# Batch 0's first-stage results: moved inside SBUF instead of through memory, and x laid out in two runs

## The chip, the cores and the metric

The kernel runs on one core of a Trainium2 chip (trn2). The metric is the device time of one execution in microseconds (us); lower is better. The kernel before takes 2643.61 us, the median of three runs from 2640.65 to 2645.09. The core has a matrix engine (PE, with PEld for its weight loads), three elementwise engines (DVE, ACT, POOL) and SP, which only issues DMA transfers; ACT can issue them too.

## The reference

The input x is 8 batches of 3008 rows of 256 numbers. Cut to what matters, the reference computes:

```python
X = np.fft.rfft(x, axis=1)
Yr = Xr @ w_r - Xi @ w_i + b_r
Yi = Xr @ w_i + Xi @ w_r + b_i
Y = sign(Y) * max(|Y| - 0.01, 0)          # on Yr and Yi apart
y = np.fft.irfft(Y, n=3008, axis=1)       # 24064 rows of 256
h = y @ moe_w_in                          # 256 to 2048
out = (h * clip(h + 3, 0, 6) / 6) @ moe_w_out   # 2048 to 256
```

So every batch passes a transform along its rows, a complex 256x256 product with a threshold, the transform back, and all rows then pass a two-layer network whose weights come as 64-bit floats.

## The kernel before, in words

**The transform** is split as 3008 = 64 x 47. `stage1(b)` does the 47-point part on TensorE. Its tiles hold 120 partitions: five of the 64 indices n1 by 24 values of k (`J` = 5, `NK` = 24, `R47` = 120). The 64 indices come in seven sets (`SEGS`): six of ten (two groups of five side by side, 512 columns) and one of four (96 partitions, 256 columns), which goes first. For each set `load` fetches the rows of x and their mirrored rows into `xin`, one vector operation forms the sum `e`, one the difference, and one matmul each (c = 0 and c = 1) gives a result that ACT copies into the tile `a` (line 303). Line 305 writes `a` to `scr1`, a buffer in memory whose axes are (c, n1), k and the 256 columns.

`middle(b)` takes the same data the other way round: for each pair g of two k values (12 pairs) `load` reads `bt`, 128 partitions (c, n1) by 2 x 256, back out of `scr1` (line 367), and a piece `f` of the 64-point transform (line 368). `s2` multiplies (line 376) and splits the result into `X` (line 131 in `split`, ACT the high part, DVE the low), `s3` does the complex product with bias and threshold, four small transfers `zt` swap halves (line 439), `s5` transforms back, and `scr2` takes the result (line 456). `segment` does the 47-point part back, `prepare` makes the operands `yb` of the network.

**The network** is done in chunks of 512 rows and eight bands of 256 hidden columns (`nf` = 8), in the main loop at the end: `phase_a` to `phase_d` (seven products per block, line 137), `gate`, and `down` (line 631). From the second batch on, `stage1` and `middle` run in small steps between these blocks. Batch 0 has nothing to hide behind: its `stage1` and `middle` stand ahead of the main loop.

**The weights** of a band are decoded on the chip from 64-bit words: `in_band(f)` and `out_band(f)` load `st` (line 178) and work on DVE, ACT and POOL (lines 190 to 222). `in_band(f)` writes its seven 128x128 blocks, as a high and a low part, into entry f of the two tiles `w_in_hi` and `w_in_lo` (`win_s`). Five bands are asked for beside `middle(0)` (`EARLY`), the others behind it with working space borrowed from tiles of `middle` (`LATE`; `bt` is one).

**What sets the order.** The program's order gives each engine's instructions a priority, and a scheduler then places them by times of its own, so the rows of an engine do not stand as the functions are written. Each engine works its row strictly in turn. Transfers issued by SP and by ACT share eight semaphores: an issue waits until the transfer eight places before it has landed. A tile with one buffer (`a` in batch 0 has seven under different names) is written again only when its last reader is done.

Of the kernel before, what the change touches and what calls it, by code (L numbers as in the profile page):

```python
# [9 lines left out]
F32 = mybir.dt.float32  # L10
F32R = mybir.dt.float32r
# [10 lines left out]
B, S, D, FF = 8, 3008, 256, 2048  # L22
N1, N2 = 64, 47
NK = N2 // 2 + 1
LAM = 0.01
P = 128

J = 5
SEGS = tuple((n1, min(2 * J, N1 - n1)) for n1 in range(0, N1, 2 * J))
R47 = J * NK  # L30
# [70 lines left out]
def spectral_ffn(ctx: ExitStack, tc: tile.TileContext, x, w_r, w_i, bias, w_in, w_out, f47, f64, g64, sgn, out):  # L101
    nc = tc.nc
    const = ctx.enter_context(tc.tile_pool(name="const", bufs=1))
    sb = ctx.enter_context(tc.tile_pool(name="sb", bufs=1))
    dram = ctx.enter_context(tc.tile_pool(name="dram", bufs=2, space=DRAM))
# [8 lines left out]
    def space(shape, dt, name, tag=None):  # L114
        tag = tag or name
        return sb.tile(shape, dt, name=name, tag=tag, bufs=depth.get(tag, 1))

    def twin(shape, dt, name, tag=None):

        t = space([P, 2, *shape[1:]], dt, name, tag)  # L120
        return t[:, 0], t[:, 1]
# [6 lines left out]
    def split(hi, lo, src, on=None):  # L128

        nc.scalar.copy(out=hi, in_=src)  # L130
        (on or nc.vector).tensor_tensor(out=lo, in0=src, in1=hi.bitcast(F32), op=ALU.subtract)  # L131

    def product(ps, terms, start=True, stop=True, more=False):

        todo = [p for (ah, al), (bh, bl) in terms for p in ((al, bh), (ah, bl), (ah, bh))]
        for n, (a, b) in enumerate(todo):
            nc.tensor.matmul(  # L137
                out=ps,
                lhsT=a,
                rhs=b,  # L140
                start=start and n == 0,
                stop=stop and n == len(todo) - 1,
                skip_group_check=more,
            )
# [13 lines left out]
    nf = NFT // 2  # L158
# [5 lines left out]

    win_s = [const.tile([P, nf, 7, P], F32R, name="w_in_" + t) for t in ("hi", "lo")]
    wout_s = [const.tile([P, NFT * D], F32R, name="w_out_" + t) for t in ("hi", "lo")]

    top = const.tile([P, 2], F32, name="top")  # L170
# [3 lines left out]
    def decode(src, cut, tags):  # L174


        st = space([P, 2, 256, 2], I32, "st", tags[0])
        nc.sync.dma_start(out=st.rearrange("p a c w -> p a (c w)"), in_=cut(src, 2))
        yield
        high = st[:, :, :, 1]  # L180
        e = space([P, 2, 256], I32, "e", tags[1])
        m, r = (
            twin([P, 2, 256], I32, "m", tags[2])
            if len(tags) == 3
            else [space([P, 2, 256], I32, n, t) for n, t in zip("mr", tags[2:])]
        )
        mf, rf = m.bitcast(F32), r.bitcast(F32)
        v, s = nc.vector, nc.scalar

        v.tensor_scalar(out=e, in0=high, scalar1=20, scalar2=0x7FF, op0=ALU.arith_shift_right, op1=ALU.bitwise_and)  # L190
        v.tensor_scalar(out=m, in0=high, scalar1=0xFFFFF, scalar2=0xFFFFF, op0=ALU.bitwise_and, op1=ALU.bitwise_and)
        yield
        s.activation(out=rf, in_=e, func=AF.Relu, bias=top[:, :1], scale=-1.0)
        s.activation(out=e, in_=rf, func=AF.Relu, bias=top[:, 1:], scale=-(2.0**23))
        v.scalar_tensor_tensor(out=e, in0=high, scalar=-(1 << 31), in1=e, op0=ALU.bitwise_and, op1=ALU.bitwise_or)
        halves = st.rearrange("p a c w -> p (a c w)").bitcast(U16).rearrange("p (a c w) -> p a c w", a=2, w=4)
        s.activation(out=rf, in_=halves[:, :, :, 1], func=AF.Copy, bias=1.0, scale=2.0**-36)
        yield
        v.scalar_tensor_tensor(out=mf, in0=m, scalar=2.0**-20, in1=rf, op0=ALU.mult, op1=ALU.add)
        nc.gpsimd.tensor_tensor(out=mf, in0=mf, in1=e.bitcast(F32), op=ALU.mult)  # L200
        return mf, e.bitcast(F32)

    def in_band(f, tags):
        def cut(t, words):
            v = t.rearrange("p (h c) -> p h c", h=2)
            return v[:, :, f * 256 * words : (f + 1) * 256 * words]

        w, s = yield from decode(w_in, cut, tags)
        s = s.rearrange("p a (b c) -> p (a b) c", b=2)
        a11, a12, a21, a22 = w[:, 0, :P], w[:, 1, :P], w[:, 0, P:], w[:, 1, P:]  # L210
        for to, a, b, op in (
            (0, a21, a22, ALU.add),
            (1, s[:, 0], a11, ALU.subtract),
            (2, a11, a21, ALU.subtract),
            (3, a12, s[:, 1], ALU.subtract),
        ):
            nc.gpsimd.tensor_tensor(out=s[:, to], in0=a, in1=b, op=op)
        yield
        hi, lo = (t[:, f] for t in win_s)
        split(hi[:, :2], lo[:, :2], w[:, :, :P])  # L220
        split(hi[:, 2], lo[:, 2], a22)
        split(hi[:, 3:], lo[:, 3:], s)
# [39 lines left out]
    scr1, scr2 = {}, {}  # L262

    def stage1(b):
        scr1[b] = dram.tile([2, N1, NK, D], F32, name="scr1")
        sets = SEGS[-1:] + SEGS[:-1]
        xins = {}

        def load(i):
            n1, n = sets[i]  # L270
            rows, w = (R47, 2 * D) if n == 2 * J else (n * NK, D)
            tag = ("xin", "gs", None, "gs", None, "raw", "raw")[i] if b == 0 else "xin"
            if tag == "gs":
                xins[i], xins[i + 1] = twin([P, 2, 2 * D], F32, "xin", tag)
            elif tag:
                xins[i] = space([P, 2, 2 * D], F32, "xin", tag)
            at = n1 // J * 2 * D
            src = x[b, :rows, at : at + 2 * w].rearrange("p (s c) -> p s c", s=2)
            nc.sync.dma_start(out=xins[i][:rows, :, :w], in_=src)
            return rows, w  # L280

        shapes = [load(i) for i in range(len(sets))] if b == 0 else [load(0)]
        for i, (n1, n) in enumerate(sets):
            rows, w = shapes[i]
            xin = xins.pop(i)
            plus, minus = xin[:rows, 0, :w], xin[:rows, 1, :w]
            e = space([P, 2 * D], F32, "e", "r" if b == 0 else "e")[:rows, :w]
            (nc.vector if b == 0 else nc.gpsimd).tensor_tensor(out=e, in0=plus, in1=minus, op=ALU.add)  # L288
            (nc.vector if b == 0 else nc.gpsimd).tensor_tensor(out=plus, in0=plus, in1=minus, op=ALU.subtract)
            for c, src in enumerate((e, plus)):  # L290
                q = 2 * i + c
                if b == 0:
                    ps = room(c == 1)
                    turns = f47_s[2][:rows, c * R47 : c * R47 + rows]
                    nc.tensor.matmul(out=ps[:rows, :w], lhsT=turns, rhs=src, start=True, stop=True)
                else:
                    xs = [t[:rows, :w] for t in twin([P, 2 * D], F32R, "xs")]
                    split(*xs, src, nc.vector if b == 1 else nc.gpsimd)
                    yield
                    ps = room()  # L300
                    product(ps[:rows, :w], [([t[:rows, c * R47 : c * R47 + rows] for t in f47_s[:2]], xs)])
                a = space([P, 2 * D], F32, "a", ("a", "h", "z", "h", "xs", "h", "X")[q % 7] if b == 0 else "a")[:rows, :w]
                nc.scalar.copy(out=a, in_=ps[:rows, :w])
                dst = scr1[b][c, n1 : n1 + n].rearrange("(g j) k d -> (j k) g d", g=w // D)
                (nc.sync if b else nc.scalar).dma_start(out=dst, in_=a.rearrange("p (g d) -> p g d", d=D))
                if c and b and i + 1 < len(sets):
                    shapes.append(load(i + 1))
                yield
# [26 lines left out]
    for i, _ in enumerate(stage1(0)):  # L335
        if i == 7:
            r, k = [loaded(w, P, 2 * D, n, "yb") for w, n in ((w_r, "w_r"), (w_i, "w_i"))]
# [14 lines left out]

    def middle(b):
        scr2[b] = dram.tile([2, N1, NK, D], F32, name="scr2")
        src = scr1[b].rearrange("c n k d -> (c n) k d")
        dst = scr2[b].rearrange("c n k d -> (c n) k d")
        NG = NK // 2
        LAG = (1, 2, 3) if b else (2, 5, 5)
        bt, xs, zs = {}, {}, {}
# [3 lines left out]
            return tags[0 if b else g % 3]  # L363

        def load(g):
            bt[g] = space([P, 2, D], F32, "bt"), space([P, 2, P], F32, "f64")
            nc.sync.dma_start(out=bt[g][0], in_=src[:, 2 * g : 2 * g + 2, :])
            nc.sync.dma_start(out=bt[g][1], in_=f64.rearrange("p (k c) -> p k c", c=P)[:, 2 * g : 2 * g + 2])

        def s2(g):  # L370
# [170 lines left out]
    WEIGHT = {1: 0, 2: 1, 3: 6, 4: 2, 5: 3, 6: 4, 7: 5}  # L541
    yb = {}
# [16 lines left out]

    def block(i, n, ps, start):  # L560
        c, f = units[i]
        product(ps, [(tuple(t[:, f, WEIGHT[n]] for t in win_s), yb[c, n])], start=start, more=True)

    def kept(i, n, ps):
        t = keep[i, n] = space([P, H], F32, n)
# [122 lines left out]
    for c in range(1, NC):  # L688
        g = prepare(c)
# [23 lines left out]
    n = len(units)  # L713
# [75 lines left out]
```

## Time and profile before

| | |
|---|---|
| median of three runs | 2643.61 us |
| the profiled execution: its own time, its span | 2643.59 us, 2641.8 us |
| PE busy, mean granted TensorE clock | 2562.4 us (97%), 0.988 |
| busy time of DVE, ACT, POOL | 1975.7, 1820.1, 796.0 us |
| last result of batch 0's stage 1 leaves ACT | 31.66 us |
| first matmul of `middle(0)` | 41.45 us |
| first `X` product of `middle(0)` | 49.98 us |
| end of its last `X` product | 107.1 us |

Times in the trace count from the start of the span. In a row of the timeline the first number is the start, the second the duration, and a square bracket tells how long the engine sat idle before and what ended that; `SPq` and `ACTq` are transfers being issued. A window row gives each engine's busy time in a stretch, then the granted clock, the busy share of the 16 DMA engines, and GB/s.

### The profile page before, as it was taken

To read this page: it belongs to the slowest core of one execution; us is meant where nothing else is said; L and a number is where in the kernel's file an instruction comes from. 1 tells how busy PE (TensorE), PEld (TensorE's weight loads), DVE (VectorE), ACT (ScalarE), POOL (GpSimd) and SP (SyncE) were. 2 spreads that over 40 slices of the span, in tenths; PEclk is the share of its full clock that TensorE was granted. 3 is DMA by queue.
4 is the path that set the end of the run, shared out by engine and by line. 5 is a ranking of instruction groups with operands and counts; after the bars stand their busy time and mean duration, and the time that the engine had idled before them with its cause. 6 is when DMAs were issued, how large, how long until landed. Compare 5 with 4: busy or idle time off the path is not lost.

```text
span 2641.8 us, 44527 instructions
## 1 busy us (share of the span) xinstructions
PE 2562.4 (97%) x16406; PEld 2291.9 (87%) x16406; DVE 1975.7 (75%) x3186; ACT 1820.1 (69%) x3592; POOL 796.0 (30%) x749
## 2 busy tenths in 40 slices
PE   5789999999999999999999999999999999999999
PEld 3577998988898998988898998999889889898887
DVE  7786886877677777777777777777777777666766
ACT  5476677767667777766776777677777666676766
POOL 2263334443233332233323333233321121121210
PEclk8889999999999999999999999999999999999999
DMA  7623333332223321323213322233221111100000
GB/s 216 191 79 93 103 104 94 113 107 75 59 60 96 88 69 48 85 78 90 73 49 86 88 76 63 76 84 84 63 79 58 50 53 53 43 26 30 12 17 17
DMA packets 150178, 199.98 MB, mean 76 GB/s; under 512 B 16847, under 2 KB 104135, under 8 KB 149959
## 3 DMA queue, kind: packets, MB, share of 16 engines
q1 hardware_dynamic: 146675, 193.98, 25.4%
q10 hardware_dynamic: 3284, 3.15, 0.4%
q8 instruction: 129, 2.11, 0.3%
q14 instruction: 90, 0.74, 0.1%
HBM read 97.45 MB, written 74.97 MB: 65 GB/s over the span
## 4 chain that ended last, share of the span: by engine, by line
PE 84%; DVE 4%; ACT 4%; DMA 2%; POOL 2%; issue 2%; SPq 0%; ACTq 0%; POOLq 0%; DVEq 0%
PE po L631 36%; PE pb L137 17%; PE ps_a L137 11%; PE pc L137 9%; PE pd L137 4%; PE ps_a L505 3%; PE ps_a L376 3%; ACT gs L130 1%; DMA xin<-in_x 1%; DVE r L610 1%; ACT r L608 1%; DVE gs L131 1%; POOL e L288 1%; DVE h L572 1%; POOL yb L131 0%
## 5 line engine op out<-in xcount | busy, mean ns | idle before, releaser
L631 PE MATMUL po<-gs,w_out_hi 128*128 128x512 f32 x3008 | 1006.5, 396 | 0.0
L610 DVE SCALAR_TENSOR_TENSOR r<-r,h 128x1024 f32<-128x1024 f32 x376 | 486.9, 1295 | 267.7 <-ACT r L608 265.9
L631 PEld LDWEIGHTS po<-gs,w_out_hi 128*128 128x128 f32 x3008 | 541.3, 188 | 85.5
L631 PE MATMUL po<-gs,w_out_lo 128*128 128x512 f32 x1504 | 601.9, 400 | 5.9 <-ACT gs L130 3.3
L608 ACT ACTIVATE r<-h,three 128x1024 f32<-128x1024 f32 x376 | 434.3, 1155 | 214.6 <-DVE h L572 211.6
L137 PE MATMUL pb<-yb,w_in_hi 128*128 128x256 f32 x3008 | 571.6, 279 | 2.5 <-POOL yb L131 2.5
L131 DVE TENSOR_TENSOR gs<-r,gs 128x1024 fp32r<-128x1024 f32 x376 | 484.4, 1288 | 80.7 <-ACT gs L130 78.8
L137 PEld LDWEIGHTS pb<-yb,w_in_hi 128*128 128x128 f32 x3008 | 461.0, 189 | 22.5 <-POOL yb L131 2.7
L130 ACT CAST gs<-r 128x1024 fp32r<-128x1024 f32 x376 | 395.8, 1053 | 92.5 <-DVE r L610 89.5
L572 DVE TENSOR_TENSOR h<-pc,u 128x256 f32<-128x256 f32 x752 | 315.1, 419 | 175.3 <-PE pc L137 160.1
L131 POOL TENSOR_TENSOR yb<-T,yb 128x256 fp32r<-128x256 f32 x188 | 181.0, 969 | 859.4 <-ACT yb L130 841.6
L137 PE MATMUL pb<-yb,w_in_lo 128*128 128x256 f32 x1504 | 431.3, 288 | 4.6 <-ACT p L567 1.6
L567 ACT COPY u<-pb 128x256 f32<-128x256 f32 x752 | 277.8, 373 | 121.5 <-PE pb L137 103.8
L631 PEld LDWEIGHTS po<-gs,w_out_lo 128*128 128x128 f32 x1504 | 284.0, 189 | 63.3 <-ACT gs L130 14.5
L137 PEld LDWEIGHTS pb<-yb,w_in_lo 128*128 128x128 f32 x1504 | 284.3, 189 | 29.7 <-ACT h L601 4.1
L137 PE MATMUL pc<-yb,w_in_hi 128*128 128x256 f32 x1504 | 297.6, 279 | 0.8 <-POOL yb L131 0.8
L137 PEld LDWEIGHTS pc<-yb,w_in_hi 128*128 128x128 f32 x1504 | 230.7, 189 | 13.3 <-POOL yb L131 1.1
L137 PE MATMUL pc<-yb,w_in_lo 128*128 128x256 f32 x752 | 219.0, 291 | 5.5 <-DVE h L572 4.9
L567 ACT COPY p<-pb 128x256 f32<-128x256 f32 x376 | 139.9, 372 | 80.9 <-PE pb L137 78.6
L601 ACT COPY h<-pb 128x256 f32<-128x256 f32 x376 | 140.5, 374 | 57.4 <-PE pb L137 55.4
L572 DVE TENSOR_TENSOR h<-pd,p 128x256 f32<-128x256 f32 x376 | 156.7, 417 | 14.9 <-ACT p L567 10.2
L137 PEld LDWEIGHTS pc<-yb,w_in_lo 128*128 128x128 f32 x752 | 142.1, 189 | 21.7 <-DVE h L572 7.9
(125 smaller groups left out, 3928.9 us busy)
## 6 DMA issues: line engine op xcount, KB each, us to landing
bt<-scr SPq DMA_DIRECT2D x96, 256.0 KB, 2.9
scr<-pt SPq DMA_DIRECT2D x96, 256.0 KB, 2.4
zt<-tc SPq DMA_DIRECT2D x376, 64.0 KB, 2.0
out<-ot SPq DMA_DIRECT2D x94, 256.0 KB, 2.3
xin<-in_x SPq DMA_DIRECT2D x48, 480.0 KB, 4.8
qt<-scr SPq DMA_DIRECT2D x96, 240.0 KB, 3.5
scr<-a SPq DMA_DIRECT2D x84, 240.0 KB, 2.5
f<-in_f SPq DMA_DIRECT2D x96, 128.0 KB, 2.8
```

The costliest lines, as they stand in the source:

```text
L130: nc.scalar.copy(out=hi, in_=src)
L131: (on or nc.vector).tensor_tensor(out=lo, in0=src, in1=hi.bitcast(F32), op=ALU.subtract)
L137: nc.tensor.matmul(out=ps, lhsT=a, rhs=b, start=start and n == 0, stop=stop and n == len(todo) - 1, skip_group_check=more,)
L288: (nc.vector if b == 0 else nc.gpsimd).tensor_tensor(out=e, in0=plus, in1=minus, op=ALU.add)
L376: nc.tensor.matmul(out=psv[:, dh, :, u, :], lhsT=data[:, u, dh * P : (dh + 1) * P], rhs=f[:, u, :], start=True, stop=True,)
L505: nc.tensor.matmul(out=ps[:, cs * w + g * rows : cs * w + (g + 1) * rows], lhsT=qt[:rows, cs, g, dh * P : (dh + 1) * P], rhs=f47_s[2][:row ...
L567: nc.scalar.copy(out=t, in_=ps)
L572: nc.vector.tensor_tensor(out=to, in0=ps, in1=keep.pop((i, n)), op=ALU.add)
L601: nc.scalar.copy(out=hs[i][:, 1, :H], in_=pb)
L608: nc.scalar.activation(out=r, in_=h, func=AF.Relu, bias=three, scale=1.0)
L610: nc.vector.scalar_tensor_tensor(out=r, in0=r, scalar=6.0, in1=h, op0=ALU.min, op1=ALU.mult)
L631: nc.tensor.matmul(out=pos[dh], lhsT=w[:, ft * D + dh * P : ft * D + (dh + 1) * P], rhs=g[:, low, u], start=f == 0 and u == 0 and which == ...
```

## The change

For batch 0 there is no `scr1` any more. `win_s` becomes one tile of 16 entries, `w_in`: the high part of band f is entry f, its low part entry 15 - f. Entries 4 to 10 (high parts of bands 4 to 7, low parts of 7, 6 and 5) are viewed as `spread`, 128 partitions by 24 by 256, in the layout that `bt` had. Each result `a` of `stage1(0)` is sent there within SBUF: one transfer for each group of five n1, its source 120 partitions of 1 KB, its destination 5 partitions of 24 KB. The first group goes out on ACT's queue, the second on SP's. `s2` of batch 0 multiplies straight from `spread`; the twelve loads `bt` of batch 0 go. The other batches keep `scr1` and `bt`.

Apart from that, x lies in memory as two runs (rows, mirrored rows) of 16 x 256 for each of the 120 rows, so that a load of 120 x 1024 takes two pieces of 2 KB from each row, where it took one of 4 KB. This holds for all batches.

```diff
-    win_s = [const.tile([P, nf, 7, P], F32R, name="w_in_" + t) for t in ("hi", "lo")]
+    win_t = const.tile([P, 2 * nf, 7, P], F32R, name="w_in")
+    win_s = [[win_t[:, f] for f in range(nf)], [win_t[:, 2 * nf - 1 - f] for f in range(nf)]]
+    spread = win_t[:, nf // 2 : nf // 2 + 7].rearrange("p f s c -> p (f s c)").bitcast(F32)
+    spread = spread[:, : NK * D].rearrange("p (k d) -> p k d", d=D)
...
-            at = n1 // J * 2 * D
-            src = x[b, :rows, at : at + 2 * w].rearrange("p (s c) -> p s c", s=2)
+            at = n1 // J * D
+            src = x[b, :rows].rearrange("p (s c) -> p s c", s=2)[:, :, at : at + w]
...
-                (nc.sync if b else nc.scalar).dma_start(out=dst, in_=a.rearrange("p (g d) -> p g d", d=D))
+                if b:
...
+                else:
+                    for g in range(w // D):
+                        at = c * N1 + n1 + g * J
+                        queue = nc.sync if g else nc.scalar
+                        queue.dma_start(out=spread[at : at + rows // NK], in_=a[:, g * D : (g + 1) * D])
...
-            bt[g] = space([P, 2, D], F32, "bt"), space([P, 2, P], F32, "f64")
-            nc.sync.dma_start(out=bt[g][0], in_=src[:, 2 * g : 2 * g + 2, :])
+            bt[g] = space([P, 2, D], F32, "bt") if b else spread[:, 2 * g : 2 * g + 2], space([P, 2, P], F32, "f64")
+            if b:
+                nc.sync.dma_start(out=bt[g][0], in_=src[:, 2 * g : 2 * g + 2, :])
```

The instructions move with it. SP's row from the load of `bias` to the first `bt` loads stands like this before; `f` are pieces of the 64-point transform, `st` the 64-bit weights:

```order
L338 DMA bias<-in_bias 128x512
L339 DMA sgn<-in_sgn 128x24
L151 DMA g_all<-in_g 128x128
L368 DMA f_232<-in_f 128x256
L368 DMA f_236<-in_f 128x256
L178 DMA st<-in_w_in 128x2x512 x4
L178 DMA st<-in_w_out 128x1024
L367 DMA bt<-scr_95 128x512 x2
```

And in the changed kernel, over the same stretch (lines are 3 to 11 higher there):

```order
L348 DMA bias<-in_bias 128x512
L315 DMA w_in<-a 5x24x256
L349 DMA sgn<-in_sgn 128x24
L315 DMA w_in<-a 5x24x256 x2
L151 DMA g_all<-in_g 128x128
L315 DMA w_in<-a 5x24x256 x3
L379 DMA f_241<-in_f 128x256
L315 DMA w_in<-a 5x24x256 x4
L379 DMA f_243<-in_f 128x256
L181 DMA st<-in_w_in 128x2x512
L315 DMA w_in<-a 5x24x256 x2
L181 DMA st<-in_w_in 128x2x512 x3
```

The two `bt` loads are gone, and twelve moves into `spread` have come in, ten of them ahead of the first load of weights and all twelve ahead of the second.

DVE's row up to the first `X` of `middle(0)`, the last rows before it, in the kernel before (`e`, `m`, `w_in` are steps of the decoding):

```order
L190 TENSOR_SCALAR e<-st 128x512
L191 TENSOR_SCALAR m<-st 128x512
L199 SCALAR_TENSOR_TENSOR m<-m 128x512
L131 TENSOR_TENSOR w_in_lo<-m,w_in_hi 128x256
L131 TENSOR_TENSOR w_in_lo<-m,w_in_hi 128x128
L195 SCALAR_TENSOR_TENSOR e<-st,e 128x512
L190 TENSOR_SCALAR e<-st 128x512
L191 TENSOR_SCALAR m<-st 128x512
L199 SCALAR_TENSOR_TENSOR m<-m,r 128x512
L131 TENSOR_TENSOR X<-pb,X 128x2x256
```

In the changed kernel the rows from the last weight split of stage 1 (`w_i_lo`) to the first `X` are these:

```order
L131 TENSOR_TENSOR w_i_lo<-cst,w_i_hi 128x512
L193 TENSOR_SCALAR e<-st 128x512
L194 TENSOR_SCALAR m<-st 128x512
L198 SCALAR_TENSOR_TENSOR e<-st,e 128x512
L202 SCALAR_TENSOR_TENSOR m<-m,r 128x512
L193 TENSOR_SCALAR e<-st 128x512
L194 TENSOR_SCALAR m<-st 128x512
L131 TENSOR_TENSOR X<-pb,X 128x2x256
```

Before, 22 decoding instructions stand between `w_i_lo` and the first `X` (and one ahead of `w_i_lo`); now six do, so that the first `X` is the 33rd instruction of DVE's row where it was the 50th, and the twelfth and last `X` of `middle(0)` is the 121st where it was the 111th. Of the decoding, ten instructions fewer are left behind that last `X`.

More of the change, by code (lines that the diff above doesn't have):

```diff
@@ L218, in in_band @@
         yield
-        hi, lo = (t[:, f] for t in win_s)
+        hi, lo = (t[f] for t in win_s)
         split(hi[:, :2], lo[:, :2], w[:, :, :P])
@@ L264, in stage1 @@
     def stage1(b):
-        scr1[b] = dram.tile([2, N1, NK, D], F32, name="scr1")
+        if b:
+            scr1[b] = dram.tile([2, N1, NK, D], F32, name="scr1")
         sets = SEGS[-1:] + SEGS[:-1]
@@ L303, in stage1 @@
                 nc.scalar.copy(out=a, in_=ps[:rows, :w])
-                dst = scr1[b][c, n1 : n1 + n].rearrange("(g j) k d -> (j k) g d", g=w // D)
-                (nc.sync if b else nc.scalar).dma_start(out=dst, in_=a.rearrange("p (g d) -> p g d", d=D))
+                if b:
+                    dst = scr1[b][c, n1 : n1 + n].rearrange("(g j) k d -> (j k) g d", g=w // D)
+                    nc.sync.dma_start(out=dst, in_=a.rearrange("p (g d) -> p g d", d=D))
+                else:
[3 more added lines that the diff above has]
+                        queue.dma_start(out=spread[at : at + rows // NK], in_=a[:, g * D : (g + 1) * D])
                 if c and b and i + 1 < len(sets):
@@ L354, in middle @@
         scr2[b] = dram.tile([2, N1, NK, D], F32, name="scr2")
-        src = scr1[b].rearrange("c n k d -> (c n) k d")
+        src = scr1[b].rearrange("c n k d -> (c n) k d") if b else None
         dst = scr2[b].rearrange("c n k d -> (c n) k d")
@@ L365, in load @@
         def load(g):
-            bt[g] = space([P, 2, D], F32, "bt"), space([P, 2, P], F32, "f64")
-            nc.sync.dma_start(out=bt[g][0], in_=src[:, 2 * g : 2 * g + 2, :])
+            bt[g] = space([P, 2, D], F32, "bt") if b else spread[:, 2 * g : 2 * g + 2], space([P, 2, P], F32, "f64")
+            if b:
+                nc.sync.dma_start(out=bt[g][0], in_=src[:, 2 * g : 2 * g + 2, :])
             nc.sync.dma_start(out=bt[g][1], in_=f64.rearrange("p (k c) -> p k c", c=P)[:, 2 * g : 2 * g + 2])
@@ L561, in block @@
         c, f = units[i]
-        product(ps, [(tuple(t[:, f, WEIGHT[n]] for t in win_s), yb[c, n])], start=start, more=True)
+        product(ps, [(tuple(t[f][:, WEIGHT[n]] for t in win_s), yb[c, n])], start=start, more=True)
     def kept(i, n, ps):
@@ L759 @@
     half = half.reshape(B, 2, 13, R47, D).transpose(0, 3, 2, 1, 4)
-    pairs = half[:, :, :12].reshape(B, R47, 6, 2, 2, D).transpose(0, 1, 2, 4, 3, 5)
-    xp = np.zeros((B, R47, 32 * D), np.float32)
-    xp[:, :, : 24 * D] = pairs.reshape(B, R47, 24 * D)
-    xp[:, :, 24 * D : 26 * D] = half[:, :, 12].reshape(B, R47, 2 * D)
+    xp = np.zeros((B, R47, 2, 16, D), np.float32)
+    xp[:, :, :, :13] = half.transpose(0, 1, 3, 2, 4)
+    xp = xp.reshape(B, R47, 32 * D)
     pos = positions()
```

## The prediction

> **What bounds the kernel now.** I read the page first, for where PE is not busy.
>
> ```profile
> span 2641.8 us, 44527 instructions
> PE 2562.4 (97%) x16406; PEld 2291.9 (87%) x16406; DVE 1975.7 (75%) x3186; ACT 1820.1 (69%) x3592; POOL 796.0 (30%) x749
> PE   5789999999999999999999999999999999999999
> DMA  7623333332223321323213322233221111100000
> PE 84%; DVE 4%; ACT 4%; DMA 2%; POOL 2%; issue 2%; SPq 0%; ACTq 0%; POOLq 0%; DVEq 0%
> ```
>
> PE carries the chain, and its gaps stand in the first three of 40 slices, where the DMA engines are busiest too. The windows give the stages; the columns are length, busy time of PE, PEld, DVE, ACT and POOL with counts, granted clock, DMA share and GB/s.
>
> ```profile
> 4.00:16.00 12.00, 9.45 (x14) 3.74 (x14) 6.50 (x11) 1.32 (x3) 0.00 (x0) 1.00 0.99 243
> 34.00:38.00 4.00, 0.00 (x0) 0.00 (x0) 3.78 (x6) 2.87 (x6) 2.24 (x3) 0.50 1.06 382
> 49.00:102.00 53.00, 48.81 (x350) 44.44 (x351) 38.04 (x63) 24.58 (x46) 8.83 (x9) 0.95 0.54 161
> 102.00:165.00 63.00, 38.83 (x186) 31.31 (x184) 57.38 (x97) 41.68 (x87) 42.94 (x44) 0.73 0.47 137
> 300.00:2600.00 2300.00, 2288.73 (x14836) 2062.31 (x14835) 1726.97 (x2797) 1616.20 (x3197) 690.64 (x640) 1.00 0.24 69
> ```
>
> From 300 us on PE is busy for 2288.73 of 2300 us. Nothing that the change does to other engines there can gain more than that rest of 0.5%, and a delay ahead of it reaches the end in full. Before 38 us the transfers are full (share 0.99 and 1.06). From 49 to 102 us `middle(0)` runs, PE-bound with 48.81 of 53; from 102 to 165 us DVE bounds with 57.38 of 63.
>
> The start's chain is read from the timeline, in rows of ACT, SP, PE and DVE:
>
> ```profile
> 11.53 0.59 ACT L303 COPY a<-ps_a 120x512 f32<-120x512 f32 x1 [3.98 <-PE pb L295]
> 18.38 0.57 ACTq L305 DMA_DIRECT2D scr<-a  x1
> 19.00 0.58 ACT L303 COPY a<-pb 120x512 f32<-120x512 f32 x1 [6.88 <-DMA cst<-in_w_r]
> 19.43 13.75 SPq L178 DMA_DIRECT2D st<-in_w_in  x4
> 31.07 0.59 ACT L303 COPY a<-pb 120x512 f32<-120x512 f32 x1
> 37.23 0.81 SPq L367 DMA_DIRECT2D bt<-scr  x2
> 41.45 3.75 PE L376 MATMUL pb<-f,bt 128*128 128x128 f32 x16 [12.30 <-ACT m L197]
> 45.55 0.57 ACT L130 CAST X<-pb 128x512 fp32r<-128x512 f32 x1
> 49.25 0.68 DVE L131 TENSOR_TENSOR X<-pb,X 128x512 fp32r<-128x512 f32 x1
> 49.98 0.58 PE L137 MATMUL ps_a<-w_r_hi,X 128*128 128x256 f32 x1 [4.78 <-DVE X L131]
> ```
>
> The last result leaves ACT at 31.66; its write to memory lands where `bt` may be issued, 37.23; the first `bt` lands, and `s2` starts at 41.45. The releaser in its bracket is ACT's, but ACT was done with that by 40.93, so it was `bt`. So memory costs 41.45 - 31.66 = 9.8 us on this path, which the change attacks. Then PE waits 4.78 us until DVE, busy decoding, comes to the first `X` at 49.25.
>
> **The change part by part.** *The moves themselves.* These rows give the transfers' sizes and times, first the totals of ACT's queue (packets, MB), then KB of one and median us to landing:
>
> ```profile
> q10 hardware_dynamic: 3284, 3.15, 0.4%
> zt<-tc SPq DMA_DIRECT2D x376, 64.0 KB, 2.0
> st<-in_w_in SPq DMA_DIRECT2D x8, 512.0 KB, 5.3
> st<-in_w_out SPq DMA_DIRECT2D x8, 512.0 KB, 4.1
> scr<-a ACTq DMA_DIRECT2D x12, 240.0 KB, 5.0
> scr<-a ACTq DMA_DIRECT2D x2, 96.0 KB, 7.7
> ```
>
> ```profile
> bt<-scr SPq DMA_DIRECT2D x2, 256.0 KB, 4.3
> ```
>
> The 14 writes on ACT's queue are 12 of 240 KB and 2 of 96 KB in pieces of 1 KB, 12 x 240 + 2 x 96 = 3072 packets. The row has 3284; the 212 left are 12 x 15 + 2 x 16. So I read that a transfer closes with one packet for each engine that it uses, and that one of 120 rows uses 15 engines and one of 96 uses 16, equal shares of whole rows. A move into `spread` has a destination of only 5 rows, so that equal shares of whole rows leave it 5 engines of 16. The Trainium skill says the same in "DMA: Bandwidth & Descriptors", section "Why a DMA increments its semaphore by 16 and not by 1": the number of engines is the largest up to 16 that divides both sides' slowest dimension. By that rule, 5 and 120 give 5; the 15 and 16 above agree with it, and no transfer with so short a side is in this trace.
>
> The moves carry the same 3.15 MB (24 of 120 KB, 2 of 96 KB). On 5 engines that is 0.63 MB each. The rate of one engine is bounded by two windows: 382 GB/s / 16 = 23.9 GB/s at 34 to 38 us, when writes of `a` and loads of weights run, and 243 / 16 = 15.2 GB/s at 4 to 16 us, when x is loaded into 120 rows. So the moves take between 0.63 / 23.9, 26 us, and 0.63 / 15.2, 41 us. I take 41: the moves, like the loads of x, write into SBUF with engines that sit close together, and `a` went into memory. They start near 14.5: the first result of full size is ready at 12.1, and the same engines are loading x until about 17. With zt's 2.0 us for the last landing, `s2` starts at 14.5 + 41.4 + 2 = 58 instead of 41.45: +16.5, between +1.5 (at 23.9) and more than 27 (a rival, below). The 9.8 us that went through memory are gone in this, and what is late next is the moves themselves.
>
> *SP's and ACT's rows.* Twelve moves stand on SP's row, all ahead of the second load of weights, and each waits for ACT's copy and for one of the eight transfers in flight. So the weights, loaded from 19.43 on before, come after 45 us or so. Who waits is DVE with the decoding; that is priced in the next step. The moves ask for no more issues than the `bt` and line-305 transfers that go (26 for 14 + 12); an issue in this form costs more, as the weights show:
>
> ```profile
> L178 SPq DMA_DIRECT2D st<-in_w_in x8: 540/578/672, 19.4 to 136.6; - x8
> L178 SPq DMA_DIRECT2D st<-in_w_out x8: 328/338/393, 34.9 to 139.6; - x8
> ```
>
> 26 x 0.24 us is 6 us over two queues, which lies under 41 us of transfer: nothing, unless the moves are quick.
>
> *DVE's row.* The first `X` is now the 33rd instruction instead of the 50th. So the 4.78 us that PE waited fall to a cast and a split, 0.57 + 0.68 and a little for the hand-over, 1.5: -3.3. The decoding that stood before it moves behind it: between the first and the last `X` stand 47 decoding instructions instead of 20. At 38.04 / 63 = 0.60 us the 27 more are 16 us, DVE 54 us in a stretch in which PE has 49. The row is no longer covered by PE: between +1 (54 for 53) and +16 (none of it covered); I take +4, as the 15 us that DVE idled there hold nearly all of it.
>
> *The tail.* From 102 to 165 us DVE bounds, and ten decoding instructions fewer are left there (43 for 53): 10 x 57.38 / 97 = 5.9 us at most, 0 at least; I take -4.
>
> *x in 2 KB pieces.* The weights again: 512 KB in 2 KB pieces land in 5.3 us, in 4 KB pieces in 4.1. A load of x, 480 KB, would be up to 1.1 us later. At the start x is limited by rate (seven loads, 3.0 MB, at 243 GB/s), and later POOL, with 690.64 busy of 2300 us, waits for it. The bounds are +9 (eight waits for x on the chain, 1.1 each) and -2 (should short pieces go faster at the start); I take 0.
>
> The sum, against the profiled execution's own 2643.59 us (its span of 2641.8 and 1.8 around it; the median of the runs is 2643.61): +16.5 - 3.3 + 4 - 4 = +13.2, **2656.8 us**.
>
> **The rivals.** *A, the moves are hidden and the kernel is faster.* If short destinations don't confine a move, it lands like `zt` in about 2 us and the chain is the copies': 31.66 + 0.6 for an issue + 2.0, `s2` at 34.3. That is -7.1, and with -3.3 for the first `X` -10.4, 2633.2 us (the +4 and -4 cancel here too). For it: `zt` moves within SBUF in 2.0 us. Against: `zt` has 64 rows on both sides, and the count of closing packets ties engines to rows. It decides if the last move lands before about 38 us.
>
> *B, five engines at full rate.* The moves take 26 us, `s2` starts at 43: +1.5 - 3.3 = -1.8, 2641.8 us, no change that counts. For it: `a` was read at that rate at 34 to 38 us. Against: there the writes went to memory.
>
> *C, the five rows crowd each other.* The five rows of a move are neighbours. If a pair of moves (ACT's and SP's) goes one after the other, each pair in 4.3 us like `bt` in the busy start, 12 x 4.3 = 52 us, `s2` starts at 68: +27 - 3.3 = +23.7, 2667.3 us. For it: loads into 120 rows reached 243 GB/s with the engines at 0.99, when 382 was to be had elsewhere, so the place of the writing matters. Against: the two moves of a pair go to different rows. The Trainium skill bears on this in "SBUF — State Buffer", section "Door 1: The DMA port swizzle (why `[64,N]` ≈ `[32,N]`)": bandwidth depends on how many of 16 ports the partitions reach, and four neighbouring partitions share a port. By its 436 GB/s over 16 ports, four rows of 24 KB take 3.6 us, and 12 pairs 43 us, an estimate that lies between my forecast and C; the 243 against 382 agrees with it, but no row shows four writers in one place.
>
> **How the numbers follow.** The forecast (moves at x's rate, end between 2650 and 2662) has 0.43, C 0.20, B 0.17, A 0.20. About 0.2% (5.3 us) is what a measurement of this kernel can tell from no change. Slower by more than that are the forecast and C, 0.63; within it B, 0.17; faster A, 0.20. The range leaves out most of A and C's upper end: 2638 to 2672 us. As cases of both signs count, the forecast's own range is 2650 to 2662.
>
> **What would show it.** In the changed kernel's profile: the moves `w_in<-a` with a landing well above 5 us, a DMA share below 0.9 between 20 and 50 us (few engines at work), closing packets of 5 a move; the first matmul of line 387 near 58 us; DVE idle before the first `X`, then busy nearly throughout until the last; PE's gain or loss all ahead of 170 us, and 300 us to the end as long as before. Wrong would be the forecast if the moves land in 2 to 3 us and line 387 starts before 40, or if the loop behind 300 us changes its length.

## The result, and the profile after

The changed kernel takes 2670.97 us, the median of runs from 2668.46 to 2673.80; the kernel before, beside it, 2644.35 (2640.65 to 2645.44). The ratio is 1.0103, with a 95% interval of 1.0086 to 1.0121: 26.6 us slower, where 13.2 were forecast. That is outside the forecast's own range of 2650 to 2662 us, and nearer to rival C's 2667.3 than to the forecast's 2656.8. The profiled execution took 2668.46 us.

From the page: its span, busy times, the slices of PE and of the DMA engines, and ACT's queue.

```profile
span 2666.6 us, 44529 instructions
PE 2566.7 (96%) x16406; PEld 2292.8 (86%) x16406; DVE 1972.5 (74%) x3186; ACT 1819.5 (68%) x3592; POOL 783.5 (29%) x749
PE   3779999999999999999999999999999999999999
DMA  5533333333222322223213322133212111101000
q10 hardware_dynamic: 1700, 1.67, 0.2%
```

The span is 24.8 us longer. ACT's queue carries 12 moves of 120 packets and 2 of 96, 1632; the 68 that are left are 12 x 5 + 2 x 4. So a move into five rows uses five engines. The windows show them at work and the stages behind:

```profile
20.00:50.00 30.00, 9.24 (x10) 2.88 (x10) 5.63 (x9) 8.09 (x16) 0.00 (x0) 0.50 0.40 117
34.00:38.00 4.00, 0.98 (x2) 0.00 (x0) 0.57 (x1) 0.00 (x0) 0.00 (x0) 0.50 0.33 97
52.00:56.00 4.00, 0.00 (x0) 0.00 (x0) 0.76 (x2) 0.50 (x1) 0.00 (x0) 0.50 1.04 255
62.80:122.60 59.80, 49.90 (x359) 45.46 (x359) 50.93 (x90) 37.57 (x72) 23.42 (x23) 0.93 0.48 141
122.60:150.10 27.50, 9.73 (x40) 5.27 (x39) 21.00 (x41) 12.90 (x26) 10.97 (x14) 0.68 0.53 164
300.00:2600.00 2300.00, 2287.32 (x14822) 2059.95 (x14821) 1728.47 (x2800) 1611.41 (x3189) 675.44 (x638) 1.00 0.24 69
```

Where the moves run alone, from 34 to 38 us, the DMA share is 0.33, which is 5 of 16 engines kept full, and the rate 97 GB/s, 19.4 GB/s an engine. All other engines stand nearly still there. The loop from 300 us on is as before (2287.32 us of PE for 2288.73).

Now the milestones, from the timeline: SP's issues, then the first product of `s2`, the first `X` product, the row that groups the 12 `X` on DVE (shortest, median, longest in ns; first and last start), and the first product of the first segment.

```profile
43.08 0.63 SPq L181 DMA_DIRECT2D st<-in_w_in  x1
45.96 4.03 SPq L315 DMA_DIRECT2D w_in<-a  x2
50.08 2.37 SPq L181 DMA_DIRECT2D st<-in_w_in  x3
60.10 3.75 PE L387 MATMUL pb<-f,w_in 128*128 128x128 f32 x16 [25.12 <-DMA st<-in_w_in]
63.54 0.58 PE L137 MATMUL ps_a<-w_r_hi,X 128*128 128x256 f32 x1
L131 DVE TENSOR_TENSOR X<-pb,X x12: 675/684/692, 62.8 to 122.0; 128x512 fp32r<-128x512 f32 x12
150.11 3.77 PE L516 MATMUL ps_a<-f_all,qt 120*128 120x120 f32 x16 [9.78 <-DMA qt<-scr]
```

The same rows of the kernel before, as far as the prediction doesn't show them:

```profile
L131 DVE TENSOR_TENSOR X<-pb,X x12: 676/682/694, 49.2 to 101.2; 128x512 fp32r<-128x512 f32 x12
126.22 3.77 PE L505 MATMUL ps_a<-f_all,qt 120*128 120x120 f32 x16 [7.19 <-DMA qt<-scr]
```

So the delay against the kernel before is 18.65 us at the first product of `s2`, 13.56 at the first `X` product, 20.8 at the last `X` (122.0 for 101.2), 23.9 at the first segment (150.11 for 126.22) and 24.8 at the end. The last move is issued by 49.99 us, and `s2` starts 10.1 us later. The bracket of `s2` names a load of weights, but `s2` reads nothing of it: in the trace's packets the last one of 1 KB, the moves' size, ends at 59.2 us, so it was the last move that released `s2`. The first of the weights is issued at 43.08 us, where it was 19.43.

### The profile page after: what moved, and what is told of

Its sections match the earlier page's. It is cut to its first block, busy times and chain, and to the rows that moved or that the text cites. A ratio compares the mean times of both kernels' runs of the same rounds, so it can differ in the third digit from the quotient of the medians.

```text
span 2666.6 us, 44529 instructions
## 1 busy us (share of the span) xinstructions
PE 2566.7 (96%) x16406; PEld 2292.8 (86%) x16406; DVE 1972.5 (74%) x3186; ACT 1819.5 (68%) x3592; POOL 783.5 (29%) x749
## 4 chain that ended last, share of the span: by engine, by line
PE 81%; DVE 6%; DMA 5%; ACT 4%; issue 2%; POOL 1%; SPq 1%; ACTq 0%; DVEq 0%; POOLq 0%
PE po L642 36%; PE pb L137 17%; PE ps_a L137 10%; PE pc L137 9%; PE pd L137 4%; PE ps_a L516 3%; PE ps_a L387 3%; DMA xin<-in_x 2%; DVE r L621 1%; ACT gs L130 1%; ACT r L619 1%; DMA w_in<-a 1%; DVE gs L131 1%; DVE h L583 1%; DMA zt<-tc 1%
## 5 line engine op out<-in xcount | busy, mean ns | idle before, releaser
L137 PE MATMUL pb<-yb,w_in 128*128 128x256 f32 x4512 | 703.0, 282 | 5.1 <-ACT h L612 1.4
L137 PEld LDWEIGHTS pb<-yb,w_in 128*128 128x128 f32 x4512 | 629.2, 189 | 49.1 <-ACT h L612 4.6
L137 PE MATMUL pc<-yb,w_in 128*128 128x256 f32 x2256 | 392.9, 282 | 1.8 <-DVE h L583 1.6
L137 PEld LDWEIGHTS pc<-yb,w_in 128*128 128x128 f32 x2256 | 336.8, 189 | 29.8 <-DVE h L583 4.2
L137 PE MATMUL pd<-yb,w_in 128*128 128x256 f32 x1128 | 197.9, 282 | 4.9 <-DVE h L583 4.7
L137 PEld LDWEIGHTS pd<-yb,w_in 128*128 128x128 f32 x1128 | 164.8, 189 | 14.0 <-DVE h L583 6.7
L131 POOL TENSOR_TENSOR yb<-raw,yb 128x256 fp32r<-128x256 f32 x139 | 134.8, 981 | 39.9 <-ACT yb L130 39.7
L292 POOL TENSOR_TENSOR e<-xin 120x512 f32<-120x512 f32 (+1 forms) x49 | 68.6, 1399 | 255.3 <-DMA xin<-in_x 251.4
```

The source lines that it names most:

```text
L137: nc.tensor.matmul(out=ps, lhsT=a, rhs=b, start=start and n == 0, stop=stop and n == len(todo) - 1, skip_group_check=more,)
```

## The experiments

The kernels of a group were timed against the kernel before on the same chip; a time is a median, with the ratio to the kernel before. "Rest" is the time from the first segment to the end of the span, 2515.6 us before and 2516.5 after.

**x in two runs, alone.** The kernel before with the lines on x from the diff.

> The kernel before with x's two runs alone (pieces of 2 KB), the way through memory unchanged. Theory (the five engines of a move are the whole cost, and the weights that come late with them): no change, 2640 to 2649 us, line 376 still starts at 40 to 43 us. Rival (short pieces cost a part of the 26 us, up to 9 by the bound of the prediction): 5 to 9 us slower, and the waits of the elementwise engines for x are longer.

2645.99 us, ratio 1.0013 (1.0004 to 1.0022); `s2` starts at 40.19 us. Not the rival's 5 to 9.

**The moves alone.** The changed kernel without these lines.

> The changed kernel with x back in one run (pieces of 4 KB). Theory (the moves carry the whole loss): 2666 to 2676 us, line 387 starts near 60 us. Rival (x's pieces carry a part): 2660 to 2666 us, and what is missing to 2671 is found in the kernel with x's layout alone.

2673.27 us, 1.0119 (1.0105 to 1.0132); `s2` at 64.30. The moves carry the whole loss. In this kernel x's two runs are even of use to the start (60.10).

**Memory with 15 engines, memory with five.** The kernel before, its writes of batch 0 issued as the moves are:

```diff
...
+                    for g in range(w // D):
+                        at = n1 + g * J
+                        dst = scr1[b][c, at : at + rows // NK].rearrange("j k d -> (j k) d")
+                        queue = nc.sync if g else nc.scalar
+                        queue.dma_start(out=dst, in_=a[:, g * D : (g + 1) * D])
```

> The kernel before, its writes of stage 1 cut as the moves are (26 transfers of one group each, the second group on SP's queue), but into memory, where the 120 rows of a group lie one behind the other, so that 15 engines share a transfer. Theory (engines): the smaller transfers and their issues cost little, line 387's counterpart (the first matmul of s2) starts at 41 to 45 us, 2642 to 2651 us. Rival (26 issues and the place on SP's row are the cost, whatever the engines): s2 starts behind 50 us, 2655 us or more.

And for five engines `scr1` is `[2, N1, NK + 1, D]`, of which 24 k are used, and `dst` stays 5 x 24 x 256.

> The same 26 writes into memory, but each n1 has room for 25 k, so that a group's five n1 no longer lie one behind the other and a transfer's destination has five rows of 24 KB, as in the moves. Nothing goes to few partitions of SBUF. Theory (few engines): 5 closing packets for a transfer of five rows, s2 starts at 60 to 68 us (the 60 of the moves and the way back out of memory of 4 us or more), 2665 to 2685 us. Rival (SBUF's few partitions take the writes slowly): s2 starts at 41 to 47 us as with 15 engines, 2642 to 2652 us.

With 15 engines, then with five:

```profile
42.31 3.75 PE L383 MATMUL pb<-f,bt 128*128 128x128 f32 x16 [13.27 <-ACT m L197]
```

```profile
q10 hardware_dynamic: 1700, 1.67, 0.2%
36.00:40.00 4.00, 0.00 (x0) 0.00 (x0) 0.00 (x0) 0.00 (x0) 0.00 (x0) 0.50 0.34 122
52.27 3.44 PE L386 MATMUL pb<-f,bt 128*128 128x128 f32 x16 [24.39 <-DMA bt<-scr1p]
```

15 engines: 2649.35 us, 1.0025 (1.0016 to 1.0034). Five: 2657.90, 1.0063 (1.0050 to 1.0075). Few engines cost 10 us of start and 8.6 us of time, without any row of SBUF being written. But 52.27 us lies between what the two theories gave, and the five engines run at 122 / 5 = 24.4 GB/s each, where the moves had 19.4 (104 / 5 = 20.8 in the window from 36 to 40 us). So something of SBUF comes on top.

**The same bytes into 120 rows of SBUF, and into five rows that lie apart.** Both leave the changed kernel's way of moving, and change the destination; the first has `s2` multiply 120 rows, too. In both, batch 0's values no longer lie where `s2` needs them, so that its results are not the reference's:

```diff
-                        queue.dma_start(out=spread[at : at + rows // NK], in_=a[:, g * D : (g + 1) * D])
+                        queue.dma_start(out=spread[:rows, slot], in_=a[:, g * D : (g + 1) * D])
```

```diff
-                        queue.dma_start(out=spread[at : at + rows // NK], in_=a[:, g * D : (g + 1) * D])
+                        queue.dma_start(out=spread[at : at + 26 * (rows // NK) - 25 : 26], in_=a[:, g * D : (g + 1) * D])
```

> The changed kernel with the same 26 moves of the same bytes within SBUF, but each into 120 partitions of 1 KB (one k slot) in place of 5 partitions of 24 KB; s2 then multiplies 120 rows, whose contents for batch 0 are not those of the reference. Theory (five engines are the cost of the moves): 15 closing packets a move, line 387 starts at 34 to 41 us, the weights come early again, 2632 to 2646 us. Rival (a move within SBUF is slow, or ten more issues on each queue are, whatever the rows): line 387 starts behind 48 us, 2655 us or more.

> The changed kernel, every row of instructions as it was, but the five rows of a move lie 26 partitions apart in place of next to each other (batch 0's rows lie in other places than the reference's product needs). Still five engines. With the five engines writing into memory (the run before this one) the writes took 46 ns a packet of 1 KB and s2 started at 52 us; in the changed kernel the share and the rate of the window from 34 to 38 us give 56 ns a packet. Theory (neighbouring rows crowd each other a little, 10 ns a packet, 6 us over 630 packets an engine): line 387 starts at 52 to 56 us, 2661 to 2667 us. Rival (the 56 ns belong to SBUF as a destination, not to neighbours): 58 to 62 us, 2668 to 2674 us, no difference.

120 rows, then rows 26 apart:

```profile
39.85 3.76 PE L387 MATMUL pb<-f,w_in 120*128 120x128 f32 x16 [9.79 <-DMA w_in<-a]
```

```profile
30.00:34.00 4.00, 0.00 (x0) 0.00 (x0) 0.82 (x2) 0.43 (x2) 0.00 (x0) 1.00 0.34 118
52.66 3.75 PE L387 MATMUL pb<-f,w_in 128*128 128x128 f32 x16 [23.16 <-DMA st<-in_w_in]
L131 DVE TENSOR_TENSOR X<-pb,X x12: 673/682/691, 55.4 to 114.2; 128x512 fp32r<-128x512 f32 x12
```

120 rows: 2645.48 us, 1.0012 (1.0003 to 1.0021). Rows apart: 2660.06, 1.0072 (1.0059 to 1.0085). This takes the start of `s2` apart: 39.85 us with 15 engines, 12.8 more with five, 7.4 more where the five rows are neighbours. From 30 to 34 us, where only moves are on their way, rows apart give 118 / 5 = 23.6 GB/s an engine, neighbours 19.4 to 20.8. The Trainium skill has the mechanism in "SBUF — State Buffer", section "Door 1: The DMA port swizzle (why `[64,N]` ≈ `[32,N]`)": four neighbouring partitions share a port, and rows 26 apart reach five different ones. The 23.6 against 19.4 agree. The kernel with 120 rows has the joined tile `w_in`, too, so that this tile does not carry the loss.

**All moves on ACT's queue**, meant to bring the weights forward: `queue = nc.scalar` for both groups.

> The changed kernel with all 26 moves on ACT's queue, so that on SP nothing stands ahead of the weights and they load at about 20 us again. Theory (late weights cost 11 us behind the start of s2, and s2's start hangs on the five engines): line 387 starts at 58 to 63 us as in the changed kernel (the weights' bytes go over the same engines either way), the stretch from the first to the last X is 52 to 55 us, 2658 to 2666 us. Rival (the lateness of the weights costs nothing): 2668 to 2676 us. A second rival (one queue for all moves is slower, 26 issues one after another at 0.74 us): line 387 starts behind 64 us.

2683.03 us, 1.0156 (1.0143 to 1.0169). The second rival: `s2` at 70.00 us. The share from 34 to 38 us stays 0.33, but the copies into `a` stand in ACT's row behind issues that wait, and the stretch from the first to the last `X` stays 58.9 us. The first four loads of weights go out between 27.5 and 57.7 us, so that it brought only the first ones forward and doesn't tell what early weights would bring.

**Late weights in the kernel before**, first with a new tile of 8 bytes that carries the wait, then without it:

```diff
...
+        if len(lates) < 5:
+            nc.scalar.copy(out=st[:R47, 0, 0, :].bitcast(F32), in_=top[:R47])
+            lates.append(0)
         nc.sync.dma_start(out=st.rearrange("p a c w -> p a (c w)"), in_=cut(src, 2))
...
```

Here `top` is written again behind ACT's last copy of stage 1; the first version copies from a new tile `late`.

> The kernel before, with memory and 15 engines, in which only the first five loads of weights wait until the last result of stage 1 has left ACT (a copy of some columns on ACT ahead of each load; the loads then go out behind 32 us in place of 19 us). Theory (the deferred decoding is what the prediction mis-sized: +7 between the first and the last X and +4 behind it): line 376's counterpart still starts at 40 to 42 us, the first X comes 2 to 3 us earlier, the stretch from the first to the last X is 57 to 61 us for 52, and the sum is 2647 to 2656 us. Rival (decoding that comes late is hidden, the +11 come from the few engines in another way): 2638 to 2646 us, the stretch at most 54 us.

> As the run in which the first five loads of weights wait for the last result of stage 1 in the kernel before, but without the new tile of 8 bytes, which moved all tiles behind it: there PE's products with w_in_hi took 282 ns for 279 through the whole loop, and PE was busy for 2585.5 us for 2562.4, while the start up to 300 us was no longer than before. Theory (deferring the decoding costs the prediction's two terms only in part: some 3 us more of PE's idle time between the first and the last X, some 5 less behind it, and the loss of 23 us came from the tiles' places): 2638 to 2646 us, 279 ns a product. Rival (the deferral itself costs 11 us or more): 2653 us or more.

With the tile 2665.72 us, 1.0093 (1.0078 to 1.0107), nearly all of it in the loop (rest 2536.6). Without it:

```profile
19.21 14.12 SPq L183 DMA_DIRECT2D st<-in_w_in  x4
L131 DVE TENSOR_TENSOR X<-pb,X x12: 676/678/692, 46.5 to 103.0; 128x512 fp32r<-128x512 f32 x12
127.65 3.77 PE L513 MATMUL ps_a<-f_all,qt 120*128 120x120 f32 x16 [8.90 <-DMA qt<-scr]
```

2651.50 us, 1.0034 (1.0021 to 1.0046), between the two theories. The profiled execution (span 2645.8, the fastest of the five, 4 us under their median) shows the terms: first `X` 2.7 us earlier, stretch 56.5 us for 52.0 (+4.5), to the first segment 24.6 for 25.0 (-0.4), rest +2.6. In the stretch DVE works for 47.87 us where it was 37.72; behind it for 16.50 where it was 21.73, and gains nothing by that.

The edit delays less than was meant. The first load still goes out at 19.21 us, the second and third at 31.46 and 32.12 (26.46 and 29.18 in the kernel before), the fourth as before (32.77 for 32.64). In the changed kernel the first four go out at 43.08 and from 50.08 on. So this run shows what some added decoding in the stretch does, not what weights as late as the changed kernel's cost.

**Decoding taken from DVE in the changed kernel.** To POOL, in both kernels:

```diff
...
+        on = nc.gpsimd if tags[0] == "raw" else None
-        split(hi[:, 3:], lo[:, 3:], s)
+        split(hi[:, 3:], lo[:, 3:], s, on)
```

(the two other `split` of `in_band` likewise), and, by itself, behind the last `X`: `turn(EARLY if i in (0, 3, 9) else None)`.

> The changed kernel, in which the low parts of the input bands decoded beside middle(0) are formed by POOL in place of DVE (15 or so instructions, about 7 us of DVE's work off the way to the first segment). In the kernel before and in the changed one DVE does the same 88.5 us of work up to the first product of the first segment (line 505, 516); in the changed one its idle time is 24 us longer. Theory (behind the first X the decoding that the late weights left over binds, DVE busy for 50.9 of 59.8 us): the stretch from the first to the last X falls from 59 to 53 to 56 us, 2663 to 2669 us. Rival (the stretch is set by waits between engines or by PE at 49.9 us, not by DVE's work): 58 to 61 us, 2669 to 2675 us.

> The same edit on the kernel before. Theory (there the stretch has PE as its bound, 48.7 us of 52.6, and DVE's decoding holds up only the first X, by 4.8 us, and the stretch to the first segment): 1 to 4 us faster, 2638 to 2642 us. Rival (POOL, at some 1 us an instruction, becomes the one that holds up the bands): 2646 us or more.

> The changed kernel with fewer bands asked for beside middle(0) (at its steps 0, 3 and 9 and no later), so that less decoding stands between the first and the last X and more behind it. Theory (DVE's decoding binds the stretch, and behind the last X the chain over zt, pt, scr and qt binds first): the stretch is 53 to 56 us, the first segment starts at 142 to 147 us, and part of it is given back behind the segment, 2664 to 2674 us. Rival (PE and the waits bind the stretch): 58 to 61 us, 2671 us or more.

On POOL: 2674.71 us, 1.0122 (1.0108 to 1.0136), stretch 58.9; the kernel before with it 2644.67, 1.0011 (1.0002 to 1.0020). For the changed kernel these are the rival's numbers, though not for its reason: DVE's time in the stretch did not fall (50.6 us for 50.9), so that the run does not test the theory. For the kernel before it is neither forecast. A group of DVE's rows from 62 to 122 us, in the changed kernel and with the splits on POOL:

```profile
L131 DVE TENSOR_TENSOR w_out_lo<-m,w_out_hi 128x512 fp32r<-128x512 f32 x3 | 2.0, 683 | 0.0
```

```profile
L131 DVE TENSOR_TENSOR w_out_lo<-m,w_out_hi 128x512 fp32r<-128x512 f32 x3 | 3.2, 1051 | 0.5 <-ACT w_out_hi L130 0.5
```

The same instruction takes 1051 ns for 683. The Trainium skill, "SBUF — State Buffer", section "SBUF: two separate sides", says that a DVE operation with two SBUF inputs and a GpSimd operation that reads SBUF lock each other out of a shared port; this row agrees.

Fewer bands beside `middle(0)`:

```profile
L131 DVE TENSOR_TENSOR X<-pb,X x12: 678/684/692, 66.2 to 121.7; 128x512 fp32r<-128x512 f32 x12
148.36 3.77 PE L516 MATMUL ps_a<-f_all,qt 120*128 120x120 f32 x16 [7.92 <-DMA qt<-scr]
```

2672.22 us, 1.0112 (1.0099 to 1.0126). The stretch falls to 55.5 us as the theory said; the first segment starts at 148.36, just behind the range, since the first `X` came 3.4 us later; the rest is 5.8 us longer (2670.7 - 148.36 = 2522.3). The last `X` starts no earlier (121.7 us for 122.0). A late first `X` does not by itself make the stretch shorter, though: with the rows apart the first comes at 55.4 us, with all moves on ACT's queue at 72.7, and the stretch is 58.8 and 58.9. So the shorter stretch goes with less decoding in it, and what is moved behind it is paid there.

**An unused tile of 8 bytes, and batch 0's x alone.** The first is the kernel before with `const.tile([P, 2], F32, name="shift")` ahead of `decode`, set to zero once and never read; the second has x in two runs for batch 0 only; the third adds the late weights to that.

> The kernel before with an unused tile of 8 bytes per partition at that place, and nothing else. Theory (the places of the tiles in SBUF set the rate of PE's products with w_in): 2660 to 2668 us, products with w_in_hi at 282 ns, no difference ahead of 200 us. Rival (the copies and waits of that run did it): 2640 to 2646 us, 279 ns.

> The kernel before with x in two runs for batch 0 alone; the other batches' x as before. With the two runs for all batches the first X product came 2.4 us earlier and the loop lost it again. Theory (short pieces help the start and hurt, if at all, in the loop): 2637 to 2642 us. Rival (the loop gives it back whatever x's pieces): 2642 to 2648 us.

> Both together: batch 0's x in two runs and the first five loads of weights behind the last result of stage 1. If deferring the weights clears the transfers of the start for x and the writes, first X product near 45 us, 2633 to 2641 us; if the loop gives it back, 2641 to 2647 us.

The tile: 2657.91 us, 1.0059 (1.0046 to 1.0072), a little under the theory's range. Batch 0's x: 2642.36, 1.0004 (0.9995 to 1.0013), no gain. Both: 2646.10, 1.0011 (1.0002 to 1.0020). With the third the first `X` product came at 45.08 us, 4.9 earlier than before, and no time was won: the stretch took 56.5 us again. The last `X` on DVE starts at 101.2 us in the kernel before, at 103.5 with 15 engines into memory, at 101.4 with 120 rows and at 100.8 here, whether the first comes at 49.2, 51.6, 44.1 or 44.3. No version here beats the kernel before.

## Where the prediction held, and which of its steps failed

The direction and the cause that the forecast named, moves on five engines, held. Two of its steps behind the first `X` failed: the tail, put at -4 and measured at +4.0, and the cover for the decoding that moves into the stretch, put at +4 and measured at +7.2. They are 11.2 us of the 11.6 by which the profiled executions differ from the forecast; the two terms ahead of them missed by +2.15 and -1.8.

*The moves* (forecast +16.5, measured +18.65): the mechanism was right, and that the size came near is in part luck. The forecast took 15.2 GB/s an engine from 14.5 us on, 41 us. Measured alone it is 19.4, between that and B's 23.9, which makes 0.63 MB 32 us; the missing time is x, which the same five engines carry at first, and the three loads of weights issued at 50.08 us, which fill all engines from 52 to 56 (share 1.04) while the last moves are on their way. The 243 GB/s of x's loads, which the forecast and C took for a sign that a place of writing is crowded, are no such sign: those loads spread over 120 rows. C was right about neighbours, for 7.4 us of the 18.65, but not about pairs of moves in turn: that its time lies nearest to the measured one is luck.

*The first `X`* (forecast +16.5 - 3.3 = +13.2): measured +13.56. PE does not wait for it at all now, so that this term is -5.09.

*The stretch between the first and the last `X`* (forecast +4): +7.2, 59.2 us for 52.0. The step said that DVE's 15 us of idle time would take up nearly all of the added decoding. The same two stages in the kernel before, to compare with the rows from 62.80 us on above:

```profile
49.30:101.90 52.60, 48.71 (x349) 44.34 (x350) 37.72 (x63) 24.18 (x46) 8.83 (x9) 0.95 0.54 161
101.90:126.20 24.30, 9.47 (x45) 5.64 (x43) 21.73 (x39) 15.16 (x28) 9.85 (x11) 0.71 0.63 194
```

DVE's work rose by 50.93 - 37.72 = 13.2 us, and its idle time fell from 52.60 - 37.72 = 14.9 only to 59.80 - 50.93 = 8.9, as rows that wait for PE, ACT and a load stay in between. Only 6 of 13.2 were covered. What the step overlooked is where the decoding stands. It is not spread over the gaps: between the second `X` and the third, from 65.3 to 77.0 us, DVE works without a gap, most of it decoding, and PE waits for the third:

```profile
77.78 0.55 PE L137 MATMUL ps_a<-w_r_hi,X 128*128 128x256 f32 x1 [6.25 <-DVE X L131]
```

That is about as much as PE's idle time in the stretch grew, 6.0 us (59.80 - 49.90 = 9.9 for 52.60 - 48.71 = 3.9). The wait that the forecast took away ahead of the first `X` came back behind it. With fewer bands it is 3.66 us. Over the kernels with the splits on DVE the stretch follows DVE's work in it: 52 us at 37 to 38 us of work (the kernel before, 15 engines into memory), 53 to 56 at 45 (five engines into memory, fewer bands, x alone), 56 to 57 at 48 to 50 (late weights, 120 rows), 59 to 62 at 49 to 52 (moves into five rows). The decoding has steps on ACT and POOL as well, which rise and fall with it, and no run holds these apart from DVE's.

*The tail* (forecast -4): this step failed. The time from the last `X` to the first segment grew by 3.1 us (28.1 for 25.0), and 0.9 came behind it. The forecast read DVE as the bound from 102 to 165 us, from one window over two stages. Before, DVE is busy for 21.73 of 24.30 us up to the first segment, which looks like a bound, but with late weights it does 5.2 us less there and the time falls by 0.4. After, it is busy for 21.00 of 27.50 us, and PE waits for the chain of `zt`, `pt`, `scr` and `qt`. The waits of PE there, after, in us, number and longest:

```profile
PE ps_a L516 <- DMA qt<-scr: 9.8, 1, 9.8
PE pb L464 <- DVE zt L448: 8.0, 2, 5.6
```

and before:

```profile
PE ps_a L505 <- DMA qt<-scr: 7.2, 1, 7.2
PE pb L453 <- DVE zt L437: 5.6, 1, 5.6
```

Fewer decoding instructions behind the last `X` shorten no transfer. Most of the growth, 2.6 us, is in the wait for `qt`, and SP's row shows what is new there. After (the last two rows are from the chain that ended last):

```profile
139.94 0.90 SPq L181 DMA_DIRECT2D st<-in_w_out  x2
140.98 0.34 SPq L467 DMA_DIRECT2D scr<-pt  x1
140.98 5.94 DMA scr<-pt
146.99 3.07 DMA qt<-scr
```

and before:

```profile
112.30 7.69 SPq L456 DMA_DIRECT2D scr<-pt  x2
121.98 1.81 SPq L486 DMA_DIRECT2D qt<-scr  x4
```

After, two loads of weights go out just ahead of the last write of `scr`, and `qt` is issued only 6.0 us behind it; before, no load stands there, the second of the two writes goes out at 119.7 us, and `qt` is issued 2.3 us later. (`qt` itself lands faster after, in 3.1 us for 4.2.) The other kernels with two loads in this place (the moves alone, rows apart, all moves on ACT's queue) have 5.9 to 6.1 us, too. No run moved these loads by themselves.

The same as a balance, DVE's work from 4 us to the first segment, before and after:

```profile
4.00:126.20 122.20, 80.12 (x436) 60.00 (x436) 88.50 (x144) 61.56 (x115) 30.11 (x34) 0.85 0.68 205
```

```profile
4.00:150.10 146.10, 82.27 (x436) 60.59 (x436) 88.52 (x156) 63.70 (x122) 37.63 (x42) 0.76 0.55 155
```

DVE does 88.5 us of work in both, so the 23.9 us of delay are idle time of DVE: at the start it has neither x nor weights to work on while the five engines are full. This tells the size and not the cause, as DVE does not bind everywhere on the way. The forecast followed PE's start and took the decoding for something that finds room later.

The sum in spans is 18.65 - 5.09 + 7.2 + 3.1 + 0.9 = 24.8. The other 1.8 us of the 26.6 lie between the profiled executions and the medians. x's pieces, forecast at 0, cost 0.13% by themselves (interval 0.04 to 0.22%).

Not settled: whether weights loaded early would help the changed kernel (all moves on one queue brought only the first forward), which of the decoding's engines binds the stretch, and why the rest behind the first segment differs by up to 12 us between kernels whose loop is the same (2510.4 with decoding on POOL in the kernel before, 2522.3 with fewer bands in the changed one). Such a spread is as large as the terms of this sum.

## What to carry to other kernels

Before a transfer goes to few partitions, count the engines that it will use (closing packets show it) and look whether its rows are neighbours: the product behind 3.15 MB of moves started 12.8 us later with five engines than with 15, and neighbouring rows cost 7.4 more. A stage's delay is then followed not only on the engine that starts it, but on the one whose work it displaces: ask in front of which instruction that work now stands, and not only how much idle time the next stretch holds. An instruction taken out of an engine's row gains nothing where a chain of transfers ends last, whatever the busy share of a longer window says.

## What the runs showed of the hardware that was not expected

An unused tile of 8 bytes, ahead of others in SBUF, made the kernel before slower by 15.6 us (2657.91 for 2642.27, interval 1.0046 to 1.0072). The products of the main loop, with the tile and without it:

```profile
PE 2577.2 (97%) x16406; PEld 2307.4 (87%) x16406; DVE 1975.0 (74%) x3187; ACT 1824.4 (69%) x3592; POOL 795.5 (30%) x749
L137 PE MATMUL pb<-yb,w_in_hi 128*128 128x256 f32 x3008 | 582.0, 282 | 2.5 <-POOL yb L131 2.5
```

```profile
L137 PE MATMUL pb<-yb,w_in_hi 128*128 128x256 f32 x3008 | 571.6, 279 | 2.5 <-POOL yb L131 2.5
```

Three ns a product, over the whole loop, and PE is busy 14.8 us longer. The kernel with the tile `late`, of the same size in the same place, has 282 ns, too. So the place of a tile in SBUF has a price on PE. Which tile's place it is was not tried.
